# Attention and residual MLP in one kernel: row-tiled scores in batches of three units, one of them in two single banks, with filler products on TensorE

## The chip, the cores and the metric

The kernel runs on one core of a Trainium2 chip. The metric is device time in microseconds (us); lower is better. The number given for the kernel before is the median of nine runs, 308.47 us, and the nine lie between 307.52 and 310.37 us. Engines are named as in the profile: PE is TensorE, DVE is VectorE, ACT is ScalarE, POOL is GpSimd, SP is SyncE.

## The reference, cut to what matters

```python
B, H, S, D = 4, 8, 768, 64                     # attention
scores = (1.0 / np.sqrt(D)) * np.matmul(q, k.transpose(0, 1, 3, 2))
# mask: 24 x 24 blocks of 32: neighbours, the first and last block row and
# column, and 3 sampled blocks for each block row
scores = np.where(mask, scores, -1000000000.0)
scores = scores - np.max(scores, axis=-1, keepdims=True)
attn = np.exp(scores)
attn = attn / (np.sum(attn, axis=-1, keepdims=True) + 1e-09)
x = np.matmul(attn, v)                          # heads joined: [4, 768, 512]
a1 = alpha1 * x + beta1
tok = np.einsum('ts,bsd->btd', w_tok, a1)       # 768 x 768 over the tokens
u = x + lam * tok
a2 = alpha2 * u + beta2
ch = np.maximum(a2 @ w_ch1, 0.0) @ w_ch2        # 512 -> 2048 -> 512
out = u + lam * ch
```

Inputs and output are float32.

## The kernel before, in words

**Work.** Heads are taken two at a time: 16 pairs (4 batches of 4 pairs). A pair's scores are cut into nine units of 128 x 1024 values, 144 units in all. For each unit PE makes the scores (the operation `qk`), ACT takes their exp out of PSUM into one of seven tiles eT (L935, one instruction of 1024 columns), and PE multiplies slices of eT with v, extended by a column of ones, into the sums of a head (`pv`, L961; eight products of 65 columns a unit). DVE normalises a finished head (L977, L980). A pair, or two, then goes through the token mixing: DVE makes a1p, PE multiplies with the transposed w_tok (`tok`, L1179), DVE adds into x_sb (L1203) and makes ub (L1217), which is transposed into uT. When a batch is through, its channel MLP follows in two halves of 384 tokens: CH1 (L1326, groups of four products of 384 columns), a relu on ACT (L1365) or DVE (L1373), and CH2 (L1406, products of 512 columns), whose result DVE adds to x_sb (L1428) and SP stores.

**Two kinds of scores.** Pairs below T0 = 5 are "full": q and k are transposed on PE (`prep_full`, L421, with copies by DVE or ACT at L478 and L476), 24 rows of mask values are put below the 64 rows of the head, and one product of 88 rows gives masked scores (L906). From pair T0 on the scores are "row-tiled": q and k are transposed by DMAs on SP (`prep_rows`), q is also copied with its halves swapped, and each product uses 64 rows, two products on the upper and the lower half of the rows being issued one behind the other (L925). The mask is then multiplied in on DVE after the exp (L942).

**Banks.** PSUM has eight banks. Two double ones (`sps`) take a unit's scores, four single ones (`gb`) everything else: PV sums, transposes, token mixing, CH1, CH2. A row-tiled unit puts the products of one half of the rows in each bank of its double bank. Before, row-tiled units are issued in batches of two, which need both double banks (L1019 and L1020); the last unit goes alone.

**Order.** The order on every engine is not written by hand. Each step is an `Op` with a due time, the operations that it depends on, banks and buffers that it needs, and a counted duration for each engine that may do it. `Plan.run` walks through time, gives each idle engine the ready operation with the earliest due time, and issues the instructions in that order; `pin_order` keeps it. A batch of row-tiled scores is counted at 585 ns, a full unit at 437 (L1040). `GB` and `GL` say from which pools a bank may come and how many must remain free: a PV sum must leave one single bank (L264). The list SEEDS shifts the due times of a random part of the operations whose due time is below 90, once for each seed (some 15 lines before the end of the function). Loads of q, k, v and weights are issued on POOL in the order that the plan gives them, the first of v and the beta2 vector by hand.

**Start.** Before the plan begins, some steps are written out: loads of pair 0's first head on SP and ACT, index tables on POOL, a mask row by DVE and two small products (L426), casts of q and k, six transposes and their copies. Between them PE gets products that nothing reads (`keep_warm`, L388): five of 512 columns, then two and ten of 128, from a tile that DVE sets to zero (L384). Its first 288 columns are used again for the mask (L704).

Of the kernel before, what the change touches and what calls it, by code (L numbers as in the profile page):

```python
# [14 lines left out]
F16 = mybir.dt.float16  # L15
# [16 lines left out]
P = 128  # L32
# [11 lines left out]
NXB = 3  # L44
SCALE = 1.0 / 8.0
EXPB = -0.35667494
T0 = 5
FINE = 3
SEEDS = [1000001, 1000004, 1000170, 1000197, 1000202, 1000205, 1000239, 1000250, 1000252, 1000261, 1000302, 1000363, 1000478, 1000491, 1000586, 1000653]
ORD = ((0, 2, 4, 1, 3, 5), (1, 3, 5, 0, 2, 4))  # L50
HF = 3 * S
MW = HF + 256
# [23 lines left out]
def dve(n, rate=1):  # L76
    return n / 0.96 / rate + 155
# [5 lines left out]

class Op:
    def __init__(
        self, name, opts, due, emit, deps=(), after=(), need=(), uses=(), urgent=False, reads=None
    ):
# [5 lines left out]
        self.reads = reads  # L93
        self.deps = [d for d in deps if d is not None]
        self.after = [d for d in after if d is not None]
        self.need = list(need)
        self.uses = list(uses) + [k for k, _ in self.need]
        self.start = None
        self.vis = None


class Plan:
# [66 lines left out]
    def run(self):  # L169
# [13 lines left out]
        while count:  # L183
            for r in [r for r in release if r[0] <= t]:
                release.remove(r)
                self.pools[r[1]].append(r[2])
            moved = True
            while moved:
                moved = False
                best = {}  # L190
                idle = [e for e in self.free if self.free[e] <= t]
                for op in cand:
                    if op.ready > t:
                        continue
# [12 lines left out]
                    taken = {}  # L207
                    for need in op.need:
                        p = self.place(need, taken)
                        if p is None:  # L210
                            break
                        taken[p] = taken.get(p, 0) + 1
                    else:
                        for o in opts:
                            best[o[0]] = (op, o)
                if not best:
                    break
                for op in cand:
                    if op.urgent and op.ready > t:
                        for o in op.opts:  # L220
                            if o[0] in best and best[o[0]][0].due > op.due:
                                if op.ready - t < best[o[0]][1][1]:
                                    del best[o[0]]
                if best:
                    op, (e, occ, vis) = min(best.values(), key=lambda x: (x[0].due, x[0].n))
                    for need in op.need:
                        p = self.place(need, {})
                        self.slot[need[0]] = (p, self.pools[p].pop(0))
                    op.start = t
                    op.eng = e  # L230
                    self.now, self.shifted = op, False
                    if callable(vis):
                        vis = vis(self, t)
                    if self.shifted:
                        for x in cand:
                            x.ready = max([d.vis for d in x.deps] + [0])
                    op.vis = t + vis
                    if op.reads:
                        self.reader[op.reads] = (e, op.vis)
                    self.free[e] = t + (self.occ or occ)  # L240
                    self.occ = None
                    for k in op.uses:
                        self.users[k] -= 1
                        self.held[k] = max(self.held.get(k, 0), op.vis)
                        if not self.users[k]:
                            release.append((self.held[k],) + self.slot[k])
                    if op.name[0] == "exp":
                        self.exps += 1
                    cand.remove(op)
                    count -= 1  # L250
                    for h in heirs.get(id(op), []):
                        h.left -= 1
                        if not h.left:
                            h.ready = max([d.vis for d in h.deps] + [0])
# [13 lines left out]
def kernel(  # L268
# [117 lines left out]
    def keep_warm(n, w, bank=3):  # L386
        for _ in range(n):
            nc.tensor.matmul(  # L388
                gbT[bank][:, 0:w], warm[:, 0:P], warm[:, 0:w], start=True, stop=True
            )  # L390
# [63 lines left out]
    for t in vext:  # L454
# [2 lines left out]

    pl = Plan(
        dict(sps=2, gb=4, eT=NE, q=4, k=4, v=4, vx=3, qk=2, hts=2, a1p=2, ub=2, ot=2),
        dict(PE=5700, ACT=6100, DVE=5750, POOL=4000, SP=4000),  # L460
    )
    GB = [("gb", 0), ("sps", 0)]
    GL = [("gb", 1), ("sps", 0)]

    def bank(key):
        p, j = pl.slot[key]
# [120 lines left out]

        return f

    LD[("v", 0)] = landed(("v", 0), 7700)  # L590
# [36 lines left out]
    for g in range(4):  # L627
# [27 lines left out]
        170,  # L655
        36,
        lambda op: nc.vector.tensor_copy(out=be2u[:, :, 15], in_=be2T[:]),
        deps=[landed(("be2",), 7000)],
    )
    B1T = []  # L660
    LB = pl.dve(
# [7 lines left out]
    for g in range(8):  # L669
# [5 lines left out]
            )  # L675

        W2S.append(pl.dve(("w2s", g), dve(1024, 2), 52 + g, e_w2, deps=[W2[g // 2], LB]))


    MASK = []  # L680
# [3 lines left out]
    def mask_ops():  # L684
# [19 lines left out]
        few = warm[:, 0 : 12 * NBLK].bitcast(F16)  # L704

        def e_x(op):
            nc.scalar.activation(
# [162 lines left out]
    for i in range(2):  # L870
        op = pl.dve(
            ("fc", i),
            dve(384, 2),
            1 + 0.1 * i,
            lambda op, i=i: first_cast(1, i, nc.vector.tensor_copy),
            deps=[landed(("f", i), 6000 - 500 * i)],
        )
        FC1.append(op)
    ROWS = []
# [18 lines left out]
    def emit_qk_full(pi, u, key):  # L898
        i = sl(("qk", pi))
        f = u * UN  # L900
        while f < (u + 1) * UN:
# [2 lines left out]
            w = min(S - c, 512 - f % 512)  # L904
            o = f - u * UN
            nc.tensor.matmul(  # L906
                spsT[sl(key)][:, o : o + w],
                kx2[i][0:KC, a, ts(jt, P)],
                qx2[i][0:KC, a, c : c + w],
                start=True,  # L910
# [4 lines left out]
    def emit_qk_rows(pi, u, key):  # L915
        i = sl(("qk", pi))
        f = u * 512
        while f < (u + 1) * 512:
# [2 lines left out]
            w = min(S - c, 512 - f % 512)  # L921
            for r in range(2):
                rows = slice(r * D, (r + 1) * D)
                o = r * 512 + f % 512
                nc.tensor.matmul(  # L925
                    spsT[sl(key)][:, o : o + w],
                    kd[i][rows, h, g, :],
                    qx2[i][rows, h, c : c + w],
                    start=True,
# [1 line left out]
                )  # L931
            f += w

    def emit_exp(op, i, key):
        nc.scalar.activation(  # L935
            eTt[sl(("eT", i))][:], spsT[sl(key)][:], AF.Exp, bias=EXPB, scale=SCALE
        )

    def emit_mult(op, i):
        e = eTt[sl(("eT", i))][:].rearrange("p (r c) -> p r c", r=2)  # L940
# [75 lines left out]
    i = 0  # L1016
    while i < NI:
        pi, u = units[i]
        batch = [i] if pi < T0 or i + 1 == NI else [i, i + 1]  # L1019
        keys = [("sps", j) for j in batch]  # L1020
        deps = []
        uses = []
        for j in batch:
# [13 lines left out]
            deps = [] if u < 4 else deps + ROWS[:1]  # L1037
        if pi == 1:
            deps = deps + ROWS[1 : 2 if u < 4 else 3]
        occ = 437 if pi < T0 else 585  # L1040
        op = pl.pe(
            ("qk", i),
            occ,
# [1 line left out]
            e_qk,  # L1045
            deps=deps,
            after=prevq[-1:],
            need=[(key, [("sps", 0)]) for key in keys],
            uses=uses,
        )  # L1050
        prevq.append(op)
        for j, key in zip(batch, keys):
            qk_of[j] = op
            ex = pl.act(
                ("exp", j),
                act(UN),
                j,
                lambda op, j=j, key=key: emit_exp(op, j, key),
                deps=[op],
                after=[EXP.get(j - 1)],  # L1060
                need=[(("eT", j), [("eT", 0)])],
                uses=[key],
            )
            EXP[j] = ex
            last = ex
# [433 lines left out]
```

## Time and profile before

| what | us |
|---|---|
| median of nine runs | 308.47 |
| the profiled execution itself | 308.9 |
| its span in the trace | 307.1 |
| first to last matmul (start to end) | 1.2 to 304.0 |
| full scores, L906 (first and last start) | 6.7 to 56.1 |
| row-tiled scores, L925 (first and last start) | 62.6 to 236.5 |
| exps, L935: 144 of mean | 1.02 |
| mask products, L942: 99 of mean | 0.685 |

The span runs from the first instruction to the last in one execution; 1.8 us of the profiled execution lie around it. A row of the page's groups gives line, engine, operation and tiles, how many instructions there were, and then their busy time in us, the mean duration of one in ns, and the engine's idle time just ahead of them with what ended it. Matmuls overlap in PE's pipeline, so the duration of one (381 ns for 512 columns of L925) is longer than the time after which the next one starts; how long PE is taken by something is read from start to start. The records of 27 matmuls of L1406 are missing from the trace.

Where the time goes by line, with the largest busy times of the page:

| line, engine | what | count | busy us |
|---|---|---|---|
| L935 ACT | exp of a unit | 144 | 139.6 |
| L1326 PE | CH1 | 512 | 96.0 |
| L1406 PE | CH2 | 373 recorded | 89.1 |
| L942 DVE | mask product | 99 | 66.2 |
| L961 PE | PV | 1152 | 55.4 |
| L1179 PE | token mixing | 360 | 34.9 |
| L925 PE | row-tiled scores | 264 | 30.1 |
| L906 PE | full scores | 120 | 27.3 |

### The profile page before, as it was taken

The numbers are of one execution on the slowest core, as the hardware profiler recorded it, in microseconds if no ns is written. First come the engines' busy times: TensorE is split into PE (matmuls) and PEld (weight loads), VectorE is DVE, ScalarE is ACT, GpSimd is POOL, SyncE is SP. The second block draws the span as 40 slices with busy tenths as digits, with TensorE's granted clock in tenths as the row PEclk, the third lists the DMA queues.
The fourth block names the chain that finished last, engine by engine and source line by source line (L and its number), as shares of the span: only waits on it lengthen the run. The fifth ranks groups of instructions, "written<-read, shape, count | busy, mean of one in ns | idle before, by whom it ended". The sixth has DMA issues, their size and how long they took to land.

```text
span 307.1 us, 7084 instructions
## 1 busy us (share of the span) xinstructions
PE 299.1 (97%) x2932; PEld 182.8 (60%) x2959; DVE 232.5 (76%) x438; ACT 179.5 (58%) x220; POOL 44.9 (15%) x71
## 2 busy tenths in 40 slices
PE   7999999999999999999999999999999999999995
PEld 4678787756475556565665565556645665555543
DVE  7689799999779878777888698878975665555531
ACT  2998998898567755798486856867668210000000
POOL 9555352231202010101000000000000000000000
PEclk9999999999999999999999999999999999999999
DMA  7999999999469765673433325213121031100011
GB/s 168 189 237 223 205 203 200 164 195 143 97 101 153 90 125 97 142 136 45 86 88 64 91 59 102 63 48 65 37 51 36 34 70 51 37 34 34 34 70 68
DMA packets 52304, 31.77 MB, mean 103 GB/s; under 512 B 29416, under 2 KB 48688, under 8 KB 52272
## 3 DMA queue, kind: packets, MB, share of 16 engines
q0 software_dynamic: 17520, 15.47, 32.3%
q1 hardware_dynamic: 34428, 15.45, 22.0%
q8 instruction: 23, 0.38, 0.6%
q10 hardware_dynamic: 324, 0.39, 0.4%
q14 instruction: 9, 0.07, 0.1%
HBM read 30.78 MB, written 6.29 MB: 121 GB/s over the span
## 4 chain that ended last, share of the span: by engine, by line
PE 91%; ACT 4%; issue 1%; DMA 1%; DVE 1%; ACTq 0%
PE gb L1326 27%; PE gb L1406 27%; PE gb L961 11%; PE gb L1179 10%; PE sps L925 9%; PE sps L906 4%; ACT eT L935 4%; PE gb L421 2%; DMA k2f<-in_k_dram 1%; DVE qk L478 0%; PE gb L388 0%; ACTq L353 0%; ACT relp L416 0%; PE gb L693 0%; DVE vext L999 0%
## 5 line engine op out<-in xcount | busy, mean ns | idle before, releaser
L935 ACT ACTIVATE eT<-sps 128x1024 f16<-128x1024 f32 x144 | 139.6, 1023 | 44.1 <-PE sps L925 36.9
L1326 PE MATMUL gb<-uT,w1b 128*128 128x384 bf16 (+1 forms) x512 | 96.0, 326 | 0.0
L1406 PE MATMUL gb<-w2b,hts 128*128 128x512 bf16 (+2 forms) x373 | 89.1, 370 | 2.0 <-issue 0.8
L942 DVE TENSOR_TENSOR eT<-eT,msk 128x1024 f16<-128x1024 f16 x99 | 66.2, 685 | 10.6 <-ACT eT L935 10.5
L1326 PEld LDWEIGHTS <-w1b 128*128 128x128 bf16 x512 | 47.3, 98 | 35.1 <-issue 3.1
L961 PEld LDWEIGHTS <-eT 128*128 128x128 f16 x1152 | 48.1, 97 | 21.1 <-issue 5.0
L1406 PEld LDWEIGHTS <-hts 128*128 128x128 bf16 x400 | 36.0, 98 | 35.7 <-issue 2.6
L961 PE MATMUL gb<-vext,eT 128*128 128x65 f16 x1152 | 55.4, 193 | 0.8 <-DVE vext L999 0.6
L1373 DVE TENSOR_SCALAR hts<-gb,b1t 128x384 bf16<-128x384 f32 x61 | 37.5, 616 | 23.5 <-PE gb L1326 22.9
L1365 ACT ACTIVATE hts<-gb,b1t 128x384 bf16<-128x384 f32 x67 | 38.4, 583 | 22.5 <-PE gb L1326 19.4
L1179 PE MATMUL gb<-a1p,wtokT 128*128 128x256 bf16 (+1 forms) x360 | 34.9, 251 | 0.0
L1179 PEld LDWEIGHTS <-wtokT 128*128 128x128 bf16 x360 | 29.2, 98 | 4.6 <-issue 0.8
L925 PE MATMUL sps<-qk 64*128 64x256 bf16 (+1 forms) x264 | 30.1, 326 | 0.0
L906 PE MATMUL sps<-qk 88*128 88x512 bf16 (+1 forms) x120 | 27.3, 336 | 0.4
L1428 DVE TENSOR_TENSOR ot<-x_sb,gb 128x512 f32<-128x512 f32 (+2 forms) x25 | 16.6, 663 | 12.8 <-PE gb L1406 12.6
L1203 DVE TENSOR_TENSOR x_sb<-x_sb,gb 128x512 f32<-128x512 f32 (+1 forms) x26 | 16.6, 643 | 5.6 <-PE gb L1179 5.4
L980 DVE TENSOR_TENSOR x_sb<-gb,rcp 128x384 f32<-128x384 f32 x32 | 17.8, 557 | 1.1
L925 PEld LDWEIGHTS <-qk 64*128 64x128 bf16 x264 | 8.9, 94 | 14.6 <-issue 11.5
L1217 DVE TENSOR_TENSOR ub<-x_sb,a_bc 128x512 bf16<-128x512 f32 (+1 forms) x26 | 16.5, 646 | 0.5
L547 POOL DMA_DIRECT2D q<-in_q_dram x15 | 10.9, 727 | 39.5 <-DMA qk<-q 32.8
L547 POOL DMA_DIRECT2D v<-in_v_dram x15 | 10.6, 705 | 38.6 <-DVE vext L999 30.7
L1141 DVE TENSOR_TENSOR a1p<-a1p,b_bc 128x768 bf16<-128x768 bf16 (+1 forms) x17 | 15.4, 905 | 0.2
(69 smaller groups left out, 131.4 us busy)
## 6 DMA issues: line engine op xcount, KB each, us to landing
out_dram<-ot SPq DMA_DIRECT2D x23, 256.0 KB, 2.2
v<-in_v_dram POOLq DMA_DIRECT2D x16, 192.0 KB, 8.7
q<-in_q_dram POOLq DMA_DIRECT2D x15, 192.0 KB, 8.6
k<-in_k_dram POOLq DMA_DIRECT2D x15, 192.0 KB, 8.6
w1b<-in_moe_w_ch_dram POOLq DMA_DIRECT2D x4, 512.0 KB, 11.7
w2b<-in_moe_w_ch_dram POOLq DMA_DIRECT2D x4, 512.0 KB, 13.6
qk<-qk SPq DMA_DIRECT2D x20, 96.0 KB, 2.5
wtk<-in_moe_w_tok_dram POOLq DMA_DIRECT2D x3, 384.0 KB, 10.0
```

The source lines that it names most:

```text
L547: nc.gpsimd.dma_start(ld[w][sl(key)][:], pair_ap(src, b, n))
L906: nc.tensor.matmul(spsT[sl(key)][:, o : o + w], kx2[i][0:KC, a, ts(jt, P)], qx2[i][0:KC, a, c : c + w], start=True, stop=True,)
L925: nc.tensor.matmul(spsT[sl(key)][:, o : o + w], kd[i][rows, h, g, :], qx2[i][rows, h, c : c + w], start=True, stop=True,)
L935: nc.scalar.activation(eTt[sl(("eT", i))][:], spsT[sl(key)][:], AF.Exp, bias=EXPB, scale=SCALE)
L942: nc.vector.tensor_tensor(out=e, in0=e, in1=msk[:, :, x : x + 512], op=ALU.mult)
L961: nc.tensor.matmul(bk[:, t * VW : t * VW + D + 1], eTt[sl(("eT", i))][:, ts(col, P)], vx[:, a, jt, 0 : D + 1], start=(r == 0), stop=(r >= ...
L980: nc.vector.tensor_tensor(out=x_sb[:, s0 : s0 + NT, h * D : (h + 1) * D], in0=o[:, :, 0:D], in1=rc[:].unsqueeze(2).broadcast_to([P, NT, D] ...
L1179: nc.tensor.matmul(bank(bk)[:, j * wp * P : (j + 1) * wp * P], wtokT[:, s, ts(m * g + j, P)], a1p[sl(ak)][:, s, 0:wp, :].rearrange("p w c ...
L1326: nc.tensor.matmul(bank(bk)[:, 0 : HS + w0], w1b[:, dk, ts(f, P)], rhs[dk], start=(dk == 0), stop=(dk == 3),)
L1365: nc.scalar.activation(htsT[hk][:, f, :], bank(bk)[:, w0 : HS + w0], AF.Relu, bias=b1t[:, f : f + 1], scale=1.0,)
L1373: nc.vector.tensor_scalar(out=htsT[hk][:, f, :], in0=bank(bk)[:, w0 : HS + w0], scalar1=b1t[:, f : f + 1], scalar2=0.0, op0=ALU.add, op1=A ...
L1406: nc.tensor.matmul(bank(ck)[:, cs], htsT[hk][:, nk, ts(mt, P)], w2h["t"][:, nk, cs], start=(nk == 0), stop=(nk == 15),)
```

## The change

Row-tiled scores are issued in batches of three units. The first unit of a batch takes two single banks in place of a double one, and its exp is two instructions of 512 columns; the other two take the double banks as before. While a batch is ready and both double banks are free, operations due later get no bank (`hold`). The counted cost of a batch is 850 ns, and a PV sum may take the last single bank. T0 becomes 6, so pair 5 is full and the 90 units left for row-tiling make 30 batches of three. The plan gets 24 filler products of 128 columns with late due times, each taken where PE is idle and more than two single banks are free. The products that nothing reads come from a constant of ones that the program sets up anyway, in place of a tile set by DVE, and six of 512 columns come first instead of five. The first part of w_tok is due at -4 instead of 0, the times at which the plan lets the engines start and first data land are changed by up to half a microsecond or so (one of the casts' by 0.85), and the seeds are others, 63 for 16, and move all due times below 300. Nothing that is computed for the output changes.

```diff
-T0 = 5
+T0 = 6
-SEEDS = [1000001, 1000004, ... 16 seeds]
+SEEDS = [3000002, 3000003, ... 63 seeds]
+NFILL = 24
...
+                held = [(o.due, o.n) for o in cand if o.hold and o.ready <= t and len(self.pools["sps"]) == 2]
+                held = min(held) if held else None
                 for op in cand:
                     if op.ready > t:
                         continue
+                    if held and op.need and (op.due, op.n) > held:
+                        if any(n[1][0][0] in ("gb", "sps") for n in op.need):
+                            continue
...
-    warm = wk.tile([P, 512], BF, name="warm", tag="warm")
-    nc.vector.memset(warm[:], 0.0)
+    some = wk.tile([P, 12 * NBLK], F16, name="some", tag="some")
+    ones = nc.const_aps.tensor(1.0, [P, 512], BF)
...
-    keep_warm(5, 512)
+    keep_warm(6, 512)
...
-        dict(PE=5700, ACT=6100, DVE=5750, POOL=4000, SP=4000),
+        dict(PE=6200, ACT=6200, DVE=6250, POOL=4000, SP=4000),
...
-    GL = [("gb", 1), ("sps", 0)]
+    GL = [("gb", 0), ("sps", 0)]
...
-        WT.append(load(("wtk", g), 2500, g, emit_wtk(g)))
+        WT.append(load(("wtk", g), 2500, (-4, 1, 2)[g], emit_wtk(g)))
...
+    for n in range(NFILL):
+        key = ("fill", n)
+        last = pl.pe(
+            key,
+            pe(1, P),
+            1000 + n,
+            lambda op, key=key: keep_warm(1, P, bank(key)),
+            after=[last],
+            need=[(key, [("gb", 2)])],
+        )
...
+    def half(key, r):
+        return spsT[sl(key[0])][:, ts(r, 512)] if len(key) == 1 else bank(key[r])
+
     def emit_exp(op, i, key):
-        nc.scalar.activation(
-            eTt[sl(("eT", i))][:], spsT[sl(key)][:], AF.Exp, bias=EXPB, scale=SCALE
-        )
+        e = eTt[sl(("eT", i))]
+        if len(key) == 1:
+            parts = [(e[:], spsT[sl(key[0])][:])]
+        else:
+            parts = [(e[:, ts(r, 512)], bank(key[r])[:]) for r in range(2)]
+        for out_, in_ in parts:
+            nc.scalar.activation(out_, in_, AF.Exp, bias=EXPB, scale=SCALE)
...
-        batch = [i] if pi < T0 or i + 1 == NI else [i, i + 1]
-        keys = [("sps", j) for j in batch]
+        batch = [i] if pi < T0 else [i, i + 1, i + 2]
+        keys = [[("sps", j)] for j in batch]
+        if len(batch) > 1:
+            keys[0] = [("sps", i, 0), ("sps", i, 1)]
...
-        occ = 437 if pi < T0 else 585
+        occ = 437 if pi < T0 else 850
...
-            need=[(key, [("sps", 0)]) for key in keys],
+            need=[(key, [("sps" if len(ks) == 1 else "gb", 0)]) for ks in keys for key in ks],
             uses=uses,
+            hold=len(batch) > 1,
...
-                act(UN),
+                act(UN) if len(key) == 1 else 2 * act(512) - 93,
...
-            if r.random() < part and op.due0 < 90:
+            if r.random() < part and op.due0 < 300:
                 op.due = due + r.gauss(0, step)
```

The products inside a row-tiled unit are the same ones as before; only the bank that each half of the rows goes to is looked up through `half`.

More of the change, by code (lines that the diff above doesn't have):

```diff
@@ L46 @@
 EXPB = -0.35667494
-T0 = 5
+T0 = 6
 FINE = 3
-SEEDS = [1000001, 1000004, 1000170, 1000197, 1000202, 1000205, 1000239, 1000250, 1000252, 1000261, 1000302, 1000363, 1000478, 1000491, 1000586, 1000653]
+SEEDS = [3000002, 3000003, 3000005, 3000006, 3000008, 3000027, 3000041, 3000052, 3000078, 3000097, 3000108, 3000114, 3000122, 3000127, 3000136, 3000180, 3000188, 3000206, 3000215, 3000219, 3000250, 3000263, 3000275, 3000280, 3000283, 3000293, 3000304, 3000326, 3000332, 3000343, 3000367, 3000440, 3000558, 3000615, 3000616, 3000621, 3000657, 3000851, 3000855, 3000993, 3001011, 3001012, 3001029, 3001046, 3001124, 3001231, 3001486, 3001568, 3001676, 3001731, 3001993, 3002553, 3003152, 3003308, 3003443, 3004176, 3005076, 3005643, 3006518, 3007963, 3008413, 3008734, 3008895]
+NFILL = 24
 ORD = ((0, 2, 4, 1, 3, 5), (1, 3, 5, 0, 2, 4))
@@ L85, in __init__ @@
     def __init__(
-        self, name, opts, due, emit, deps=(), after=(), need=(), uses=(), urgent=False, reads=None
+        self, name, opts, due, emit, deps=(), after=(), need=(), uses=(), urgent=False, reads=None, hold=False
     ):
@@ L93, in __init__ @@
         self.reads = reads
+        self.hold = hold
         self.deps = [d for d in deps if d is not None]
@@ L381, with keep_warm @@
     nc.gpsimd.dma_start(ld["v"][0][:], pair_ap(v, 0, 0))
-    warm = wk.tile([P, 512], BF, name="warm", tag="warm")
-    nc.vector.memset(warm[:], 0.0)
-    def keep_warm(n, w, bank=3):
+    some = wk.tile([P, 12 * NBLK], F16, name="some", tag="some")
+    ones = nc.const_aps.tensor(1.0, [P, 512], BF)
+    def keep_warm(n, w, to=gbT[3]):
         for _ in range(n):
-            nc.tensor.matmul(
-                gbT[bank][:, 0:w], warm[:, 0:P], warm[:, 0:w], start=True, stop=True
-            )
-    keep_warm(5, 512)
+            nc.tensor.matmul(to[:, 0:w], ones[:, 0:P], ones[:, 0:w], start=True, stop=True)
+    keep_warm(6, 512)
     def where(out, what, op, lim):
@@ L588, in emit_w2 @@
         return f
-    LD[("v", 0)] = landed(("v", 0), 7700)
+    LD[("v", 0)] = landed(("v", 0), 7500)
     pl.slot[("v", 0)] = ("v", 0)
@@ L657 @@
         lambda op: nc.vector.tensor_copy(out=be2u[:, :, 15], in_=be2T[:]),
-        deps=[landed(("be2",), 7000)],
+        deps=[landed(("be2",), 6500)],
     )
@@ L677 @@
         W2S.append(pl.dve(("w2s", g), dve(1024, 2), 52 + g, e_w2, deps=[W2[g // 2], LB]))
+    last = None
+    for n in range(NFILL):
[8 more added lines that the diff above has]
+        )
     MASK = []
@@ L703, in mask_ops @@
         )
-        few = warm[:, 0 : 12 * NBLK].bitcast(F16)
+        few = some[:]
         def e_x(op):
@@ L875 @@
             lambda op, i=i: first_cast(1, i, nc.vector.tensor_copy),
-            deps=[landed(("f", i), 6000 - 500 * i)],
+            deps=[landed(("f", i), 5000 + 1350 * i)],
         )
@@ L906, in emit_qk_full @@
             nc.tensor.matmul(
-                spsT[sl(key)][:, o : o + w],
+                spsT[sl(key[0])][:, o : o + w],
                 kx2[i][0:KC, a, ts(jt, P)],
@@ L923, in emit_qk_rows @@
                 rows = slice(r * D, (r + 1) * D)
-                o = r * 512 + f % 512
+                o = f % 512
                 nc.tensor.matmul(
-                    spsT[sl(key)][:, o : o + w],
+                    half(key, r)[:, o : o + w],
                     kd[i][rows, h, g, :],
@@ L932, in emit_qk_rows @@
             f += w
+    def half(key, r):
+        return spsT[sl(key[0])][:, ts(r, 512)] if len(key) == 1 else bank(key[r])
     def emit_exp(op, i, key):
-        nc.scalar.activation(
-            eTt[sl(("eT", i))][:], spsT[sl(key)][:], AF.Exp, bias=EXPB, scale=SCALE
-        )
+        e = eTt[sl(("eT", i))]
[5 more added lines that the diff above has]
+            nc.scalar.activation(out_, in_, AF.Exp, bias=EXPB, scale=SCALE)
     def emit_mult(op, i):
@@ L1061 @@
                 need=[(("eT", j), [("eT", 0)])],
-                uses=[key],
+                uses=key,
             )
```

## The prediction

> **What bounds the kernel now.** I read the page first, for the busy shares and the chain, then the stretches, to see whether one bound holds throughout.
>
> ```profile
> span 307.1 us, 7084 instructions
> ## 1 busy us (share of the span) xinstructions
> PE 299.1 (97%) x2932; PEld 182.8 (60%) x2959; DVE 232.5 (76%) x438; ACT 179.5 (58%) x220; POOL 44.9 (15%) x71
> ...
> PE 91%; ACT 4%; issue 1%; DMA 1%; DVE 1%; ACTq 0%
> ```
>
> ```profile
> 10.00:60.00 50.00, 48.80 (x753) 38.87 (x752) 43.40 (x96) 45.48 (x51) 22.23 (x32) 1.00 1.25 207
> 60.00:240.00 180.00, 178.30 (x1781) 104.36 (x1802) 147.10 (x265) 127.13 (x160) 14.06 (x20) 1.00 0.49 91
> 240.00:304.00 64.00, 63.69 (x362) 35.16 (x366) 34.74 (x56) 2.58 (x5) 0.00 (x0) 1.00 0.14 48
> ```
>
> The columns after the stretch's length are PE, weight loads, DVE, ACT, POOL. PE leads everywhere; ACT comes near it only in 10 to 60 us (45.5 of 50), where all its exps are of full units. As a busy PE need not be PE at its peak, I then read the PE timeline and laid the start of each group against the start of the next:
>
> ```profile
> 69.83 0.61 PE L925 MATMUL sps<-qk 64*128 64x256 bf16 x6
> 70.37 3.42 PE L1326 MATMUL gb<-uT,w1b 128*128 128x384 bf16 x20
> 73.72 0.61 PE L925 MATMUL sps<-qk 64*128 64x512 bf16 x6
> 74.26 1.67 PE L961 MATMUL gb<-vext,eT 128*128 128x65 f16 x48
> 75.77 0.38 PE L1406 MATMUL gb<-w2b,hts 128*128 128x512 bf16 x1
> ```
>
> The 48 PV products take 75.77-74.26 = 1.51 us, 31 ns each. A CH1 product (L1326) is followed after 162 ns where another follows, but the 20 here take 3.35 us, 0.10 more than 20 x 162.5. Over all matmuls, the last one before a row-tiled batch (L925) is late by 96 ns whatever kind it is (258 for 162, 312 for 216, 126 for 30), and a batch's own last pair is followed 93 ns late. Inside, two products of the two row halves start 3 ns apart and a pair takes 223 ns (512 columns) or 109 ns (256). This is 189 ns for a batch, the same for batches of two, four and six matmuls. From 60 us on I find nothing else between matmuls than this and products whose record is missing. So PE's own work is the time there, and what a change adds to or takes from it is the change's worth.
>
> In 10 to 57 us there are waits besides, about 3.0 us in a dozen gaps of 0.1 to 0.3 us, nearly all before a score product (L906) whose double bank an exp still holds. One, at 39.59: four PV products need 0.12 us and the next scores start 0.40 later.
>
> ```profile
> 38.91 1.02 ACT L935 ACTIVATE eT<-sps 128x1024 f16<-128x1024 f32 x1 [0.15 <-ACT eT L935]
> ...
> 39.59 0.28 PE L961 MATMUL gb<-vext,eT 128*128 128x65 f16 x4
> ...
> 39.99 0.59 PE L906 MATMUL sps<-qk 88*128 88x512 bf16 x2
> ```
>
> And one wait of 0.74 us at the start: the first PV stands still until v is copied.
>
> ```profile
> 10.45 0.46 DVE L999 COPY vext<-v 128x768 f16<-128x768 f16 x1
> ...
> 10.96 0.65 PE L961 MATMUL gb<-vext,eT 128*128 128x65 f16 x16 [0.58 <-DVE vext L999]
> ```
>
> **Batches of three.** Before, 99 units go in 50 batches (49 pairs, one single); after, 90 units in 30 batches of 8 matmuls. Twenty switches fewer at 189 ns: -3.78 us. The Trainium skill ("TensorEngine Tiling (Array Packing)", Key Properties) says that a change of tiling mode drains TensorE; it gives no price, the row does.
>
> **Pair 5 goes untiled.** Its nine units were 12 pairs of row-tiled products, 6 x 223 + 6 x 109 = 1.99 us; as full ones they are 12 x 216 + 12 x 109 = 3.90 us: +1.91. Its q and k are now transposed on PE, 12 x 56 = +0.67. The same page (Theoretical Speedup) speaks against this: up to 2x is given away for a contraction of 64 rows or fewer. By the rule nine units would double, +1.99. By the row a tiled unit costs 0.22 + 0.189/2 = 0.32 us in batches of two against 0.43, a factor of 1.4; the switches saved stand in the part above. Either way it is an addition. Beside it DVE loses nine mask products (L942, 9 x 685 = 6.2 us) and two swaps (0.7) and gains two copies of 0.55, ACT two of 0.79; SP loses three transposing DMAs. These lie beside PE: DVE is at 147 of 180 us in the middle stretch. Without that cover the copies would cost 2.7 us.
>
> **Sum of PE's work:** -3.78 + 1.91 + 0.67 = -1.20 us.
>
> **The split exp.** Thirty units are exponentiated in two halves. No 512-wide exp is in the trace; the nearest rows are 128x288 (408 ns) and 128x1024 (1023 ns), a straight line between them gives 595. Two halves: 1.19 for 1.02, so +0.17 x 30 = 5.0 us of ACT, from zero (if the fixed part overlaps) to that. ACT has 53 us idle in 60 to 240 us: I take nothing for it; uncovered it would be the 5.0.
>
> **Start.** The memset of the warm tile (0.27 us on DVE) goes, and PE's warm-up can start that much sooner with six products for five. What PE needs then is k's first half (landed 4.76, cast by 5.29) and the mask row; neither moves, so the first scores stay at 6.7. Here the skill's clock rule ("TensorE: Matmul & The Clock Gate", Part 1) is worth weighing: about 3.4 us of sustained work bring full speed. In the trace spacing is 107 ns for 128 columns until about 9.3 us and 56 after, 8 us after the first product. By the rule an unbroken warm-up could bring this one window forward and halve 6.7 to 9.3, -1.3 us. By the row it does not: the gaps at 3.8, and 4.69 to 5.35 (waiting for k's cast) have no filler in the new order either. I take 0, with -1.3 as the low end.
>
> Of the 24 fillers, PE's new order has five before unit 5, and 19 behind the last CH2. The 19 (19 x 56 = 1.1 us) run while DVE stores and the last DMA lands, 3.1 us between PE's last product (304.0) and the span's end: 0; if they held the end, +1.1. Four of the five come while the clock is low, 4 x 107 = 0.43 us, before unit 2's scores, which waited for nothing in the trace: +0.2 (0 to +0.5). On DVE v's copy now comes ahead of pair 0's two copies; v landed at 7.87, so the 0.74 wait goes, and what is late next is exp 1 (done at 9.74), which the new order reaches no sooner than 9.8. Start together: -0.5.
>
> **Loads and waits to 60 us.** On POOL the first token weights (384 KB) move ahead of k and q of pair 1, and the other two ahead of v of pair 1. Loads land about 1 us per 192 KB in that stretch, so q1 comes at about 11.8 for 9.9 and v1 at about 16.6 for 11.8. PE's order takes q1 and k1 only after pair 0's unit 6 (two exps in a row take 1.94 us in the timeline, from 7.8 on, so 13.6 or later), and v1 with unit 9 (after 17.5). Two us of slack and one: 0 taken, up to +2. The plan's start times of engines and its cost of a tiled batch (585 ns for what takes 635; now 850 for what adds up to 2 x 223 + 2 x 109 + 189 = 853) are nearer to the trace, and products of CH1 stand among the last full units to fill gaps. Against that the tight stage is nine units longer (exps of 54 units for 45). Waits of 3.0 us: between all gone (-3.0) and half as many again (+1.5). I take -0.5, since the same two buffers feed the same exp.
>
> **The order elsewhere.** The other seeds, the holding back of takers of banks while a batch waits, and a PV sum's right to the last single bank act only through the order: the same CH1, CH2, token and PV products in 369 runs of one kind for 407. A change between two untiled kinds costs nothing in the trace (162, 216 or 31 ns as inside a run), so fewer runs bring nothing: 0 for PE's work, and what goes wrong would be a wait, taken up under the banks below.
>
> **Sum:** -1.20 - 0.5 - 0.5 = -2.2 us. The profiled execution (308.9, span 307.1) would become 306.7; on the median of 308.47, 306.3 us.
>
> **Rivals.** *Work only (307.3, 0.20).* Neither start nor waits improve: -1.2. For it: orders searched against a plan tend to gain less than planned.
> *Waits mostly gone (304.4, 0.13).* -1.2 - 0.5 - 2.4. For it: more PE work for each exp in units 45 to 53.
> *Late loads (308.4, 0.12).* v1 or q1 lands 2 us later than I reckon, PE stands still for it and gives the gain back: -2.2 + 2.1.
> *Banks run short (311.9, 0.12, slower).* A batch of three holds both double banks and two of four single ones, and two PV sums can hold the others. All eight are then taken until the two half exps are read, 1.2 us, and PE has at most three units of PV for it (24 x 31 = 0.74): 0.5 us bare, 0.8 with a handover as ahead of the last store's addition on DVE (0.34 idle), and I take 0.7 for each such batch in 72 to 235 us. The tiling page's Gotcha 1 (PSUM pressure) points here. From four batches on it eats the 2.2; at eight of thirty it is +5.6. Against it: the trace has no PE wait there with four single banks, and in the new order 16 of 30 batches are followed at once by CH1 or CH2, which must own a bank.
> *The switch isn't saved (311.1, 0.03).* If the 189 ns grew with the batch, only +2.6 would remain. Three batch sizes with one price speak against it.
>
> **Numbers.** The forecast has 0.40. What a measurement can tell from no change is about 0.3%, 0.9 us. Forecast, work only and waits gone are faster by more (0.73); late loads is the same (0.12); banks short and no saving are slower (0.15). Range 304.0 to 308.8: from waits gone to late loads, with the slower cases left out.
>
> **What would show it.** Row-tiled matmuls 240 in 30 groups of 8, each 0.85 us from the end of the product before to the next; the late 96 and 93 ns seen 30 times; nothing but these from 75 to 235 us (else banks); PE's last product near 301.8; v's copy before 8.5 and no wait ahead of the first PV; waits to 70 us of about 2.5 us. Wrong if the clock turns at 5.9 (low end), if PE waits for gb behind a batch, or if transposes of pair 1 wait for DMA.

## The result, and the profile after

The changed kernel takes 306.3 us in the median of 16 runs (305.67 to 308.63), the kernel before 308.7 in 53 runs on the same chips (307.45 to 311.53). The ratio is 0.9916, 95% interval 0.9896 to 0.9936: 2.6 us faster (2.0 to 3.2) by the ratio, 2.4 by the two medians. The forecast was 306.3.

The profiled execution does not show this at first sight. It took 308.65 us, a little above the slowest of the 16, against 308.9 in the profile before. The page's head and chain:

```profile
span 306.9 us, 7168 instructions
## 1 busy us (share of the span) xinstructions
PE 300.4 (98%) x2970; PEld 188.9 (62%) x2996; DVE 228.9 (75%) x434; ACT 179.7 (59%) x246; POOL 44.5 (15%) x71
...
PE 89%; ACT 7%; DMA 1%; issue 1%; DVE 1%; ACTq 0%
```

And the stretches (after the length: PE, weight loads, DVE, ACT, POOL):

```profile
10.00:60.00 50.00, 49.21 (x758) 39.58 (x757) 42.58 (x91) 44.83 (x50) 23.66 (x34) 1.00 1.24 209
60.00:240.00 180.00, 178.70 (x1776) 108.67 (x1793) 144.19 (x268) 128.65 (x188) 12.64 (x18) 1.00 0.50 88
240.00:304.00 64.00, 63.68 (x396) 35.90 (x401) 35.19 (x57) 2.91 (x5) 0.00 (x0) 1.00 0.14 48
```

PE is the bound in every stretch as before; DVE has 3 us less to do in the middle one, ACT 1.5 more. The exps stand on the page so, the whole and the half ones:

```profile
L962 ACT ACTIVATE eT<-sps 128x1024 f16<-128x1024 f32 x114 | 110.8, 1031 | 8.1 <-PE sps L924 7.3
...
L962 ACT ACTIVATE eT<-gb 128x512 f16<-128x512 f32 x60 | 32.5, 595 | 32.7 <-PE gb L943 32.6
```

Halves take 595 ns, the straight line's figure, but two of them start so close that 60 keep ACT busy for 32.5 us, 1.08 for two: the split costs 0.06 us, not 0.17, for each unit (1.08 against 1.02 for a whole one). A batch of three in PE's timeline:

```profile
99.57 0.29 PE L986 MATMUL gb<-vext,eT 128*128 128x65 f16 x4
99.79 0.39 PE L943 MATMUL gb<-qk 64*128 64x512 bf16 x2
100.01 0.60 PE L943 MATMUL sps<-qk 64*128 64x256 bf16 x6
100.54 0.60 PE L1434 MATMUL gb<-w2b,hts 128*128 128x512 bf16 x2
```

Four PV products are worth 0.12 us and take 0.22, and the eight tiled products take 0.75 (755 to 757 ns in 28 of the 30 batches; the other two stand before a wait and before a product whose record is missing).

These rows also correct the prediction's price of a switch. A batch of one 512-column pair and two of 256 columns took 540 ns before (73.72 to 74.26 in the prediction's lines). The batch here is the same with one more 512-column pair and takes 756. So a 512-column pair inside a batch costs 216 ns, as much as an untiled product of 512 columns; the prediction's 223 comes from the first pair of a batch, which is slower. Counted with 216 and 109, every batch, before and after, spends 107 ns beyond its pairs, besides the 96 ns by which it comes late: 0.20 us, not 0.189. The untiled product behind a batch is mostly followed some 10 ns late as well (226 for 216, 173 for 162), which makes it 0.21.

Why, then, is the span nearly that of before? The start. The same kernel's second profile (a_again) has a span of 303.5 us, and the two differ ahead of the first full scores (L924). First after:

```profile
5.95 0.51 ACT L421 CAST relp<-k2f 128x384 bf16<-128x384 f32 x1 [2.41 <-DMA k2f<-in_k_dram]
...
6.51 0.50 PE L426 MATMUL gb<-identb,relp 128*128 128x128 bf16 x3 [1.63 <-ACT relp L421]
6.80 1.27 PE L395 MATMUL gb<-const-bfloat16-1.0 128*128 128x128 bf16 x10
7.87 1.91 PE L924 MATMUL sps<-qk 88*128 88x512 bf16 x5
```

Then a_again:

```profile
5.14 0.34 PE L426 MATMUL gb<-identb,relp 128*128 128x128 bf16 x3 [0.79 <-ACT relp L421]
5.32 0.75 PE L395 MATMUL gb<-const-bfloat16-1.0 128*128 128x128 bf16 x10
5.92 0.89 PE L924 MATMUL sps<-qk 88*128 88x512 bf16 x4
```

In the first, k's first half landed at 5.92 us instead of 4.55, and ten products of 128 columns fill 1.07 us (107 ns each) where in the second they fill 0.60 (56 to 60 each). I call the doubled spacing the low clock and the moment at which it ends the clock's turn. It is read from the spacing alone: the page's column for the granted clock shows 1.00 in these microseconds too. The low clock lasted to about 12.7 us in the one and was over at 3.9 in the other.

To set runs beside each other in spite of this, I cut PE's time in the same way in each profile. From the first full scores to the start of the last CH2 product I add all start-to-start times; what a product takes longer than its kind usually does is a wait (above 22 ns), the double spacing of the start is "low clock", the rest is PE's work, switches included. A gap that fits a product whose record is missing counts as work.

| kernel (us) | first scores at | low clock | waits to 14 us | waits 14 to 75 | waits 75 to 240 | batches | work |
|---|---|---|---|---|---|---|---|
| before | 6.71 | 1.36 | 0.84 | 2.94 | 0 | 50 | 291.90 |
| b_again | 6.51 | 1.35 | 0.87 | 2.79 | 0 | 50 | 291.90 |
| after | 7.87 | 2.18 | 0.07 | 2.63 | 0.37 | 30 | 290.63 |
| a_again | 5.92 | 0.23 | 0.60 | 2.68 | 0.28 | 30 | 290.65 |

Work is reproduced to 0.02 us and is 1.26 us less, whatever the start does.

One more piece lies behind these columns. From the start of the last CH2 product to the end of the span it is 3.39 to 3.43 us in all four profiles with the order of before, and 3.12 and 3.09 in the two of the changed kernel: 0.3 us less at the end. Of the ten profiles of the changed kernel and its variants eight show this (3.08 to 3.12). Why the end is shorter stays open; the fillers are not the reason, since without them (a_nofill2, below) it is 3.09.

### The profile page after: what moved, and what is told of

Read it like the earlier page. It is cut to its first block, busy times and chain, and to the rows that moved or that the text cites. A ratio compares the mean times of both kernels' runs of the same rounds, so it can differ in the third digit from the quotient of the medians.

```text
span 306.9 us, 7168 instructions
## 1 busy us (share of the span) xinstructions
PE 300.4 (98%) x2970; PEld 188.9 (62%) x2996; DVE 228.9 (75%) x434; ACT 179.7 (59%) x246; POOL 44.5 (15%) x71
## 4 chain that ended last, share of the span: by engine, by line
PE 89%; ACT 7%; DMA 1%; issue 1%; DVE 1%; ACTq 0%
PE gb L1434 27%; PE gb L1354 27%; PE gb L1207 10%; PE gb L986 10%; ACT eT L962 6%; PE sps L924 5%; PE sps L943 4%; PE gb L943 3%; DMA k2f<-in_k_dram 1%; PE gb L426 1%; PE gb L395 1%; DVE eT L967 1%; ACTq L360 0%; DVE x_sb L1005 0%; DVE hts L1401 0%
## 5 line engine op out<-in xcount | busy, mean ns | idle before, releaser
L962 ACT ACTIVATE eT<-sps 128x1024 f16<-128x1024 f32 x114 | 110.8, 1031 | 8.1 <-PE sps L924 7.3
L1354 PE MATMUL gb<-uT,w1b 128*128 128x384 bf16 (+1 forms) x512 | 93.7, 326 | 0.0
L967 DVE TENSOR_TENSOR eT<-eT,msk 128x1024 f16<-128x1024 f16 x90 | 59.2, 683 | 5.4 <-ACT eT L962 5.4
L986 PEld LDWEIGHTS <-eT 128*128 128x128 f16 x1152 | 49.0, 98 | 18.4 <-issue 3.7
L1393 ACT ACTIVATE hts<-gb,b1t 128x384 bf16<-128x384 f32 x64 | 36.7, 583 | 27.3 <-PE gb L1354 24.2
L962 ACT ACTIVATE eT<-gb 128x512 f16<-128x512 f32 x60 | 32.5, 595 | 32.7 <-PE gb L943 32.6
L1401 DVE TENSOR_SCALAR hts<-gb,b1t 128x384 bf16<-128x384 f32 x64 | 39.3, 615 | 15.4 <-PE gb L1354 14.4
L924 PE MATMUL sps<-qk 88*128 88x512 bf16 (+1 forms) x144 | 33.2, 337 | 0.5 <-ACT eT L962 0.2
L1005 DVE TENSOR_TENSOR x_sb<-gb,rcp 128x384 f32<-128x384 f32 x32 | 17.8, 557 | 1.1
L943 PE MATMUL sps<-qk 64*128 64x256 bf16 x180 | 17.9, 305 | 0.0
L1158 DVE TENSOR_TENSOR a1p<-x_sb,a_bc 128x768 bf16<-128x768 f32 (+1 forms) x17 | 15.4, 905 | 0.2
```

The source lines that it names most:

```text
L924: nc.tensor.matmul(spsT[sl(key[0])][:, o : o + w], kx2[i][0:KC, a, ts(jt, P)], qx2[i][0:KC, a, c : c + w], start=True, stop=True,)
L943: nc.tensor.matmul(half(key, r)[:, o : o + w], kd[i][rows, h, g, :], qx2[i][rows, h, c : c + w], start=True, stop=True,)
L962: nc.scalar.activation(out_, in_, AF.Exp, bias=EXPB, scale=SCALE)
L967: nc.vector.tensor_tensor(out=e, in0=e, in1=msk[:, :, x : x + 512], op=ALU.mult)
L986: nc.tensor.matmul(bk[:, t * VW : t * VW + D + 1], eTt[sl(("eT", i))][:, ts(col, P)], vx[:, a, jt, 0 : D + 1], start=(r == 0), stop=(r >= ...
L1005: nc.vector.tensor_tensor(out=x_sb[:, s0 : s0 + NT, h * D : (h + 1) * D], in0=o[:, :, 0:D], in1=rc[:].unsqueeze(2).broadcast_to([P, NT, D] ...
```

## The experiments

**a_again: the changed kernel once more.** No edit.

> The changed kernel once more, for its ratio and for a second look at its start. In its first profile k's first half was cast late and PE stood still for 1.9 us ahead of k's transposes (0.77 in the profile before), the first full scores began at 7.87 us instead of 6.71, and the short spacing of the products came at 12.4 instead of 9.3. Theory (the gain lies behind the start, in PE's own work, and the start is a lottery of the run): median near 306.3, about 0.8% below the kernel before; if k comes early in this profile, the span is about 304 and PE's way from the first full scores to the last CH2 product about 1 us shorter than in the first profile only by the low clock. Rival (the changed start costs 1 us in each run): the first scores begin near 7.9 again.

306.69 us against 308.87, ratio 0.9924 (0.9900 to 0.9948). The first scores came at 5.92, so the late start of the first profile was that run's and the rival falls. But the clock turned at 3.9 us, sooner than I had held possible.

**b_again: the kernel before once more.** No edit.

> The kernel before once more, for a second look at its start and its waits. Theory: PE's way from the first full scores to the last CH2 product, less waits and the low clock, is 291.9 us as in its first profile (290.6 in three profiles of the changed order), with 50 switches of 189 ns and about 3 us of waits from 14 to 75 us; the wait ahead of the first PV is there again. Rival (the 1.3 us between the two kernels are scatter): it falls to 291.2 or below.

308.62 us in one run; work 291.90, to the hundredth that of the first profile, and the wait ahead of the first PV is there again (0.87 up to 14 us). The 1.26 us are no scatter.

**a_switch: sixty more switches in the same order.**

```diff
             for j, key in zip(batch, keys):
                 pj, uj = units[j]
+                if j > batch[0]:
+                    keep_warm(1, 24, spsT[sl(key[0])])
```

> The changed kernel in its own order, with an untiled product of 24 columns put ahead of the second and the third unit of each batch, into the bank that the unit overwrites: the batch of three is cut into three row-tiled runs, 90 for 30, and nothing else moves. Theory (189 ns for each run, paid on PE, and PE's work is the time): 60 x (0.189 + 0.03) = +13.1 us, about 319.5. Rival (part of it fills waits that are there anyway, or a run that follows at once costs less): +3 to +10.

320.72 us, ratio 1.0386 (1.0361 to 1.0411), 14.4 us above the changed kernel's median, and by the profiles 303.86 us of work for 290.64: +13.2 for the 13.1 expected. (Some 0.3 us more are waits behind 14 us, and 0.3 the end.) One batch in its timeline:

```profile
104.39 0.39 PE L943 MATMUL gb<-qk 64*128 64x512 bf16 x2
104.71 0.19 PE L395 MATMUL sps<-const-bfloat16-1.0 128*128 128x24 bf16 x1
104.83 0.39 PE L943 MATMUL sps<-qk 64*128 64x256 bf16 x4
105.15 0.19 PE L395 MATMUL sps<-const-bfloat16-1.0 128*128 128x24 bf16 x1
105.27 0.39 PE L943 MATMUL sps<-qk 64*128 64x512 bf16 x2
105.59 0.42 PE L986 MATMUL gb<-vext,eT 128*128 128x65 f16 x8
```

The first pair is left after 0.32 instead of 0.22 us, and the product of 24 columns after 0.12 instead of 0.03. A switch costs this at each of the 60 places, and nothing fills it. With the price of 0.21 us the 24 columns would be worth some 10 ns and not the 30 that I counted; this run gives only the sum of the two, 0.22.

**a_single: one unit at a time.**

```diff
-        batch = [i] if pi < T0 else [i, i + 1, i + 2]
+        batch = [i]
...
-        occ = 437 if pi < T0 else 850
+        occ = 437 if pi < T0 else 410
```

> The changed kernel with its 90 row-tiled units one at a time: 90 switches of tiling for 30, no split exps, counted cost 410 ns for a unit. Theory (189 ns for each batch, on the path): 60 more, +11.3 us, about 317.6, and each unit shows 0.096 before and 0.093 behind it. Rival (the gain came from the order, the switch is hidden or is paid per unit anyway): within 2 us of the changed kernel. ACT's time falls by about 5 us in either case.

318.60 us (ratio 1.0326, 1.0288 to 1.0364), near the figure, but not by the count expected: units often stood side by side, so there were 68 tiled runs where 90 were expected, 38 more than in the changed kernel, and work rose by 8.55 us: 38 x 0.20 to 0.21 = 7.6 to 8.0, and 19 of the fillers, which now stood inside PE's way (1.1). The rest are waits, 6.3 us from 14 us on where the changed kernel has 3.0. The edit also changes the number of operations in the plan, and this shifts the random change of due times for all behind it; that is why I trust a_switch, not this run.

**a_nofill: no fillers.**

```diff
-NFILL = 24
+NFILL = 0
```

> The changed kernel without the 24 filler products of the plan (five early, 19 behind the last CH2). Theory: the five lie in waits or cost 0.2 us at most, the 19 lie beside the last store; within 0.5 us of the changed kernel, the same order otherwise. Rival (fillers keep the clock up): the clock turns later or falls back, 1 us slower or more. Second rival (the fillers at the end or start cost their time): 0.5 to 1.5 us faster.

316.04 us, ratio 1.0232 (1.0195 to 1.0268). The theory and the second rival missed. The first rival named "1 us slower or more", and the clock did turn late in this profile (12.1 us), but the low clock costs 2.2 us in all there, as in the changed kernel's first profile, and cannot be the 9.7. Work is near that of the changed kernel (291.21), but PE waits 5.0 us up to 75 and 7.0 us from 75 to 240. One of those waits:

```profile
227.53 0.80 PE L943 MATMUL sps<-qk 64*128 64x256 bf16 x6
...
228.82 0.56 DVE L1005 TENSOR_TENSOR x_sb<-gb,rcp 128x384 f32<-128x384 f32 x1
...
229.43 1.30 PE L1354 MATMUL gb<-uT,w1b 128*128 128x384 bf16 x7 [1.09 <-DVE x_sb L1005]
```

CH1 stands for 1.1 us until DVE has read a finished PV sum (L1005), whose bank it needs. This is the "banks run short" rival of the prediction, in an order that nobody searched: taking 24 operations out shifts the random numbers of the seeds, so this plan has the seeds' changes at the wrong operations. That the order and not the missing fillers did it is shown by the next run.

**a_nofill2: no fillers, order kept.**

```diff
-            lambda op, key=key: keep_warm(1, P, bank(key)),
+            lambda op: None,
```

> The changed kernel in its own order, the 24 fillers planned but not issued. The first trial without fillers shifted the random changes of due times of all later operations, so it had another order, and 12 us of waits on PE for 3. Theory (fillers are worth nothing, that trial's 10 us were the order): within 0.5 us of the changed kernel. Rival (fillers keep the clock): 1 us slower or more, and the short spacing later than about one window.

306.05 us, ratio 0.9926 (0.9904 to 0.9948), the changed kernel's own figure. The fillers are worth nothing in the median; without the five that stand in PE's way its work is 290.35, 0.28 less.

**b_start and b_start2: the changed warm-up alone on the kernel before.**

```diff
-    warm = wk.tile([P, 512], BF, name="warm", tag="warm")
-    nc.vector.memset(warm[:], 0.0)
+    some = wk.tile([P, 12 * NBLK], F16, name="some", tag="some")
+    ones = nc.const_aps.tensor(1.0, [P, 512], BF)
...
-    keep_warm(5, 512)
+    keep_warm(6, 512)
```

> The kernel before with the changed warm-up alone: products from the constant, six of 512 columns for five, no memset; the plan and its order untouched. Theory (the start is limited by k's landing): same as before within 0.5 us. Rival (an earlier or longer warm-up turns the clock one window sooner): 1 us or more faster.

308.23 against 308.77, ratio 0.9974 (0.9951 to 0.9997).

> The kernel before with the changed warm-up alone, a second time: the first gave 0.26% with an interval that nearly reaches none, and a profile in which the clock turned at 5.1 us (9.6 to 9.8 in both profiles of the kernel before, 3.4 to 5.1 in four of the changed start and 8.7 to 12.7 in six). Theory (the warm-up that begins 0.4 us sooner and has a sixth product turns the clock a window sooner in about half of the executions): 0.3 to 1.3 us faster, the first scores' products 109 or 216 ns apart from the start or after about 8.7 us. Rival (the first trial was scatter): within 0.3 us.

308.21 against 308.60, ratio 0.9969 (0.9944 to 0.9993). By the ratios two trials agree on 0.8 to 1.0 us, though each interval all but reaches none and the medians lie only 0.5 and 0.4 apart. PE's start in b_start, and in b_again:

```profile
4.36 0.41 PE L419 MATMUL gb<-identb,relp 128*128 128x128 bf16 x3
5.08 0.34 PE L419 MATMUL gb<-identb,relp 128*128 128x128 bf16 x3 [0.32 <-ACT relp L414]
5.26 0.75 PE L388 MATMUL gb<-const-bfloat16-1.0 128*128 128x128 bf16 x10
5.96 1.10 PE L904 MATMUL sps<-qk 88*128 88x512 bf16 x5
```

```profile
4.37 0.53 PE L421 MATMUL gb<-identb,relp 128*128 128x128 bf16 x3
5.15 0.50 PE L421 MATMUL gb<-identb,relp 128*128 128x128 bf16 x3 [0.26 <-ACT relp L416]
5.45 1.27 PE L388 MATMUL gb<-warm 128*128 128x128 bf16 x10
6.51 1.91 PE L906 MATMUL sps<-qk 88*128 88x512 bf16 x5
```

The transposes of k begin at nearly the same time, yet the scores come 0.55 us sooner and are done in 1.1 instead of 1.9, because the clock turned at 5.1 us instead of 9.6. In b_start2's profile it turned at 9.2.

**a_gapfill: eight more products where PE waits for k.**

```diff
     for w in range(2):
+        if w:
+            keep_warm(8, P)
```

> The changed kernel with eight more products of 128 columns that nothing reads, between the transposes of q and of k, where PE waits for k's cast. Theory (the clock's turn needs unbroken work, and this gap keeps it low): [...]1 to 1.3 us faster. Rival (the turn is set otherwise[...]): the same time, or 0.1 to 0.8 us slower where k is there before the eight are through (8 x 0.107 = 0.86 us).

306.08 us, ratio 0.9917 (0.9884 to 0.9949): the same as without. In its profile the clock had turned at 3.4, ahead of the gap, so that the profile cannot tell what the eight do at a low clock; the six runs show no gain.

**a_two_s: batches of two, seeds drawn anew.** For this run and the next, a new list of seeds was found as the change's own list seems to have been: a seed is kept where the plan's counted end comes earlier.

```diff
-        batch = [i] if pi < T0 else [i, i + 1, i + 2]
+        batch = [i] if pi < T0 else [i, i + 1]
-        if len(batch) > 1:
+        if False:
             keys[0] = [("sps", i, 0), ("sps", i, 1)]
-        occ = 437 if pi < T0 else 850
+        occ = 437 if pi < T0 else 635
-            hold=len(batch) > 1,
+            hold=False,
```

> The changed kernel with batches of two (45 for 30), each counted at 635 ns, no single banks for scores and no split exp, and seeds searched anew for this plan as long as those of the changed kernel seem to have been. Theory (what the batch of three is worth is the switches): 15 x 0.189 = +2.8 us, with waits like those of the changed kernel, about 309.1. Rival (batches of two leave more banks and wait less, so that little is lost): +1 us or less, and then fewer waits than the changed kernel's 3 us.

309.81 against 309.88 (ratio 0.9997, 0.9973 to 1.0022): without the third unit in a batch the gain is gone. By the profile, work is 3.2 us more (15 switches are 2.8 at 0.189, 3.0 to 3.2 at 0.20 to 0.21), the waits 0.7 to 0.8 more: 1.65 up to 75 and a single one of 2.06 us behind it, for a copy of q's halves (issued from SP) that landed later than the plan counted:

```profile
77.67 0.81 PE L1354 MATMUL gb<-uT,w1b 128*128 128x384 bf16 x4
...
80.47 0.61 PE L943 MATMUL sps<-qk 64*128 64x512 bf16 x6 [1.99 <-DMA qk<-qk]
```

**a_t5_s: pair 5 row-tiled again, seeds drawn anew.**

```diff
-T0 = 6
+T0 = 5
```

> The changed kernel with pair 5 row-tiled again (33 batches of three), seeds searched anew for as long. Theory (PE's work is the time): -1.91 - 0.67 + 3 x 0.189 = -2.0 us, about 304.3. Rival (without the full pair PE meets waits for exp, masks or banks at the passage from full to tiled scores, since the searched order itself gets longer): the work is 2.0 less but the waits are 3 to 5 us more, 307 to 310.

307.37 us, ratio 0.9933 (0.9902 to 0.9964). Work fell by 1.7 us (2.0 expected), but the waits from 14 to 75 us rose from 2.7 to 4.9, most of the rise at the passage from full to tiled units:

```profile
62.14 2.32 PE L1354 MATMUL gb<-uT,w1b 128*128 128x385 bf16 x12 [0.53 <-ACT hts L1393]
...
64.92 0.69 DVE L967 TENSOR_TENSOR eT<-eT,msk 128x1024 f16<-128x1024 f16 x1
...
65.67 0.42 PE L986 MATMUL gb<-vext,eT 128*128 128x65 f16 x8 [0.45 <-DVE eT L967]
```

CH1 waits for a relu on ACT, PV for a mask product on DVE. Pair 5 as a full pair needs no mask products, at the time when DVE has b1's columns, the w_ch2 scaling and the first relus to do. So the extra PE work of the full pair is given back in fewer waits; that the two nearly balance holds for these two orders, since each was searched once.

**a_hot: six more seeds for the changed kernel.**

```diff
-SEEDS = [3000002, 3000003, ... 63 seeds]
+SEEDS = [3000002, 3000003, ... 63 seeds, 6000239, 6004863, 6009277, 6016604, 6016795, 6017763]
```

> The changed kernel with six more seeds, found by searching on from its own. Theory (what is left are about 3 us of waits up to 75 us, and the search takes out a part): 0.2 to 0.5 us faster than the changed kernel. Rival (the counted times are not good to 0.3 us): the same or slower.

305.93 us, ratio 0.9885 (0.9851 to 0.9918), the fastest of all, with 290.62 us of work, 2.17 us of waits up to 75 and none behind. Its lead over the changed kernel is not clear of the intervals.

## Why the prediction was right, and where it was not

The median came out at the forecast to the tenth. The largest term, PE's own work, is right and shown. That the total agrees so closely is luck: the other two terms, start and waits, were off by several tenths in opposite directions, and the 0.3 us at the end were not in the sum.

**PE's own work, -1.20: right in mechanism, a little small.** Measured -1.26 with the five early fillers in it (0.28), so -1.54 without. The difference is the price of a switch. With 0.20 to 0.21 us for each, and 216 ns for a 512-column pair, the same sum is 20 x 0.20 to 0.21 = -4.0 to -4.2, +3.90 - (6 x 0.216 + 6 x 0.109) = +1.95 for pair 5, and +0.67: -1.4 to -1.6. That each tiled run costs a fixed time wherever it stands is shown by a_switch (13.2 us for 60 runs more in the same order) and agrees with a_two_s.

**Pair 5, +2.6 of PE work and nothing else: half the story.** The work was right to 0.3 us (a_t5_s). That it also takes out waits at the passage was not in the sum; I had put DVE's 6.2 us down as hidden.

**Split exp, 0: right,** and its price was 1.8 us of ACT (30 x 0.06), not 5.0.

**Start, -0.5: the term that was mis-sized.** It had two parts. V's copy was taken at -0.5 net of the fillers. To compare starts I add the time of the first scores, the low clock and the waits up to 14 us. In the four variants of the changed kernel whose clock turned at 8.7 to 9.2 us (a_nofill2, a_single, a_t5_s, a_hot) this is 7.9 to 8.0, and 8.8 in b_start2, which has the warm-up but not the order and whose clock turned at 9.2: -0.8.

The warm-up was taken at 0, with -1.3 as the low end, because the gaps ahead of k's transposes remain. They do remain, but the prediction's sign of being wrong, a turn at 5.9 us or sooner, came in five of the twelve profiles with the new warm-up: there the clock turned at 3.4 to 5.1 us. In five it turned at 8.7 to 9.2, and in two at 12.1 and 12.7, both with k's first half landed late, at 5.02 and 5.92. Both profiles of the old warm-up show 9.6 and 9.8. On the average of executions b_start and b_start2 make it 0.8 to 1.0 us. The Trainium skill ("TensorE: Matmul & The Clock Gate", Part 1) asks for about 3.4 us of sustained work and counts it in windows that run by themselves. Turns at one of several times go with such windows better than with my reading of one trace. The 3.4 us do not go with a_gapfill, where the spacing is short from 3.43 us on, 2.65 us after the first product. Which of the two edits, the earlier first product or the sixth, moves the turn was not tried.

The two parts don't add up in one execution. Where the clock turns early, PE can wait for DVE's casts of the second halves of k and q instead: 0.96 us in a_switch, whose start comes to 7.4 by that sum, hardly less than the 7.6 of b_start with the order of before. Over the ten profiles of the changed kernel and its variants it runs from 6.8 to 10.1, 8.0 in the mean, against 8.7 and 8.9 in the two of before. So the start is worth some 0.8 us in all, with a wide scatter.

**Waits, -0.5: wrong, by a small amount.** From 14 to 75 us they went from 2.9 to 2.7, and 0.3 to 0.4 came anew behind 75. The re-counted durations of the plan did not make them fewer.

**The rivals.** Late loads did not come: the transposes of pair 1 and the PV of unit 9 do not wait for a DMA. Short banks cost little here: the waits behind 75 us are 0.3 to 0.4 in all. That they can cost more is shown by a_nofill, with 7.0 us of waits in that stretch. The searched order has next to none of these waits; with the changes of due times at other operations they are there.

**The sum.** -1.26 of work, about -0.8 of the start, -0.3 at the end, +0.1 of waits: -2.3, within the measured 2.0 to 3.2. The forecast of -2.2 had -1.2, -0.5, nothing and -0.5: what it missed at the start and at the end was covered by a gain in waits that did not come.

## What to carry to other kernels

Where one engine is full, read its timeline from start to start: a cost that no row names, such as 0.2 us for every passage into and out of row tiling, shows as a constant lateness at the seams, and fewer seams are worth that. Take the price of a product from the middle of a run: here the first one behind a seam is slower, and counting it as usual hid a part of the seam's cost. Where a planner orders the instructions, removing or adding one operation can reorder everything, so an ablation has to keep the order (plan the operation and issue nothing) or it measures the order. And one profile is one draw of the start: compare the part behind the start, or several profiles, before a difference of two microseconds is explained.

## What the runs showed of the hardware that was not expected

With a first product at 0.78 us in each of twelve profiles, the clock turned in three groups: at 3.4 to 5.1, 8.7 to 9.2, and 12.1 to 12.7 us after the start of the span. A passage into row tiling and back cost PE 0.20 to 0.21 us, with two to eight products in between. Two half exps started so close that a pair of 595 ns instructions took 1.08 us. K's first half, loaded by a DMA issued at 1.38 to 1.40 us, landed between 4.4 and 5.9 us in the 14 profiles.
